# Queries of two attention heads laid block-diagonal with zeros, one 128-row product for both heads' scores

## The chip, the cores and the metric

The kernel runs on one core of one Trainium2 chip. The metric is the device time of one execution in microseconds (us), and the figure for the kernel before is the median of three runs. Matrix products run on TensorE, whose records in the trace come in two kinds: PEld, the load of the stationary operand (the weights), and PE, the product itself, which streams the columns of the moving operand past those weights. The other engines are VectorE (DVE), ScalarE (ACT), GpSimd (POOL) and SyncE (SP), which here issues most loads.

## The reference

Attention with a causal window of 64 over 8 sequences of 576 tokens, 8 heads of 64, and behind it a mixture of 8 experts that picks one expert for each token. What is computed:

```python
scores = scale * np.matmul(q, k.transpose(0, 1, 3, 2))
rel = pos[:, None] - pos[None, :]
mask = (rel >= 0) & (rel < window)
scores = np.where(mask, scores, -1000000000.0)
attn = np.exp(scores - np.max(scores, axis=-1, keepdims=True))
attn = attn / (np.sum(attn, axis=-1, keepdims=True) + 1e-09)
x = np.matmul(attn, v)                       # to (B, S, H * D)
...
h = np.maximum(x[b, s] @ w1[e], 0.0)         # e: the expert chosen for this token
out[b, s] = p[e] * (h @ w2[e])
```

## The kernel before

The 4608 tokens are cut into nine stretches `sc` of 512 tokens (`SC`), and the 8 heads into four pairs `hp`. One `(sc, hp)` is a unit, so there are 36. For each unit `scores` (L387 on) makes S = K Q for both heads of the pair with keys on the partitions; the exponential is taken on ACT (L425), the window mask is multiplied in on DVE (L430; in the units of `BIASED` the mask is instead added by four or six short bf16 products, L409), and `values` (L432 on) multiplies with V on TensorE (L440) and divides by the sums on DVE (L445 to L450).

Head 2·hp lies on partitions 0 to 63 of the loaded tile, head 2·hp+1 on 64 to 127. So a score product contracts over 64 rows only, and the array is used as four quarters of 64 rows by 64 columns: `j` (the head) picks the rows, `c` (even or odd block of 64 keys) the columns:

```python
def one(j, c, kt, block, a, b):
    h = slice(j * DH, (j + 1) * DH)
    nc.tensor.matmul(sp[j][c * WIN:(c + 1) * WIN, a:b], lhsT=kt[h, hp, block * WIN:(block + 1) * WIN],
                     rhs=qt[h, hp, a:b], start=not biased, stop=True, skip_group_check=biased)
```

Each unit has 18 such products, which the trace shows as 36 records (two for every float32 product). `sp[j]` is one PSUM bank for each head, out of a pool of three.

The order on TensorE, ACT and SP is the order in which the code is written: scores are made two units ahead (`LEAD`), that is, in the turn of unit i the scores of i+2 come first and then the values of i. Between them stand transposes and gate products (L310, L323, L325, L340) and pieces of the router, which `step` deals out. DVE and POOL are ordered by the scheduler.

Keys and queries are loaded together: the array `kq` holds for each stretch and partition the four pairs' keys and queries side by side, one tile of 2 MB is filled in two halves by L240 on SP's queue, and lies in the pool `ring` of four buffers, which the experts' weights `w1` and `w2` use later (`weights`, L1257). `va` (L235) is V with a column of ones, `vtt` (L230) V turned around for the gates. Behind attention the experts run block by block (L1279, L1357, L1408, L1508 are their products).

Of the kernel before, what the change touches and what calls it, by code (L numbers as in the profile page):

```python
# [8 lines left out]
F32 = mybir.dt.float32  # L9
# [74 lines left out]
def kernel(  # L84
# [36 lines left out]
    xs = xs, xw  # L121
    moe = xs, (w1, w1t), w2, out, tabs, lt, ident
    with ExitStack() as fast:
        ring = fast.enter_context(tc.tile_pool(name="ring", bufs=4))
        rt = Router(fast, tc, lt, xs, tabs, ident)
        ex = Experts(fast, tc, ring, *moe)
        zeros, n = ex.xp.tile([P, D], F32, name="xg"), (ZR - T1) // HF
        nc.vector.memset(zeros[:HF], 0.0)

        def small():  # L130
            nc.gpsimd.dma_start(out=wgs, in_=wg)
            nc.gpsimd.dma_start(out=wg2s, in_=wg2)
            for i in (ZR, N + 1):
                nc.gpsimd.dma_start(out=xs[0][i:i + 1, :], in_=zeros[:1])
                nc.gpsimd.dma_start(out=xw[i:i + 1, :], in_=zeros[:1, :PW])
            nc.gpsimd.dma_start(out=xw[T1:ZR, :].rearrange("(c p) o -> p c o", p=HF),
                                in_=zeros[:HF, :n * PW].rearrange("p (c o) -> p c o", c=n))

        attention(tc, ring, kq, v3, v4, vt, vh, xs[0], lt, ok, wgs, wg2s, ident, rt, ex, small)
        ex.run(fast, rt, lambda ps: flag(nc, ps, ok, bad, tabs["ej"][:, NBLK:], rare, ident))  # L140
    if_rare = nc.values_load(rare[0:1, 0:1], min_val=0, max_val=1,  # L141
                             skip_runtime_bounds_check_because="the larger of two comparisons")
    with tc.If(if_rare > 0):
        if_bad = nc.values_load(bad[0:1, 0:1], min_val=0, max_val=1,
                                skip_runtime_bounds_check_because="the result of a comparison")
        with tc.If(if_bad > 0):
            careful(tc, q, k, v, xs[0], lt, wgs, ident)
            with ExitStack() as slow:
                ring = slow.enter_context(tc.tile_pool(name="ring2", bufs=4))
                rt = Router(slow, tc, lt, xs, tabs, ident)  # L150
                rt.prepare()
                ex = Experts(slow, tc, ring, *moe)
                with tc.tile_pool(name="rt_ps1", bufs=1, space=PSUM) as ps:
                    for _ in rt.first(lambda: ps.tile([P, SC], F32, name="a")):
                        pass
                ex.begin()
                ex.run(slow, rt)
        if_more = nc.values_load(tabs["ej"][0:1, NBLK:], min_val=0, max_val=1,
                                 skip_runtime_bounds_check_because="the larger of two comparisons")
        with tc.If(if_more > 0), ExitStack() as slow:  # L160
            ring = slow.enter_context(tc.tile_pool(name="ring3", bufs=4))
            Experts(slow, tc, ring, *moe).more(slow)


# [10 lines left out]
def attention(ctx, tc, ring, kq, v3, v4, vt, vh, xs, lt, ok, wg, wg2, ident, rt, ex, small):  # L175
# [34 lines left out]

    ctx.enter_context(tc.manual_schedule(engines={ET.PE, ET.Activation, ET.SP}))

    kqs, qts, kts, vts, vas, vbs = {}, {}, {}, {}, {}, {}

    def width(sc):
        return VW if sc in GATED else VX
# [9 lines left out]
    def load(sc, parts):  # L226
        for part in parts:
            if part == "turned":
                vts[sc] = tp.tile([P, HP, SC], F32, name="vtt")
                nc.sync.dma_start(out=vts[sc], in_=vt[GATED.index(sc)])  # L230
            elif isinstance(part, tuple):
                if sc not in vas:
                    vas[sc] = space("va", sc)
                src, h = v4[GATED.index(sc)] if sc in GATED else v3[sc], slice(*part)
                nc.sync.dma_start(out=vas[sc][:, :, h], in_=src[:, :, h])  # L235
            else:
                if sc not in kqs:
                    kqs[sc] = ring.tile([P, HP, 2, SC], F32, name="w")
                    kts[sc], qts[sc] = kqs[sc][:, :, 0], kqs[sc][:, :, 1]
                nc.sync.dma_start(out=kqs[sc][:, part], in_=kq[sc, :, part])  # L240

    late = cp.tile([1, 4], F32, name="late")

# [29 lines left out]

    colf = columns()
    masks = []

    def build_mask(i):
        m = cp.tile([P, KB, 2, WIN], F32, name=f"mask{i}")
# [106 lines left out]
        return copied  # L385

    def scores(sc, hp):  # L387
        qt, kt = qts[sc], kts[sc]
        sp = [ps_s.tile([P, SC], F32, name="sp") for _ in range(2)]
        biased = (sc, hp) in BIASED  # L390

        def one(j, c, kt, block, a, b):
            h = slice(j * DH, (j + 1) * DH)
            nc.tensor.matmul(sp[j][c * WIN:(c + 1) * WIN, a:b], lhsT=kt[h, hp, block * WIN:(block + 1) * WIN],  # L394
                             rhs=qt[h, hp, a:b], start=not biased, stop=True, skip_group_check=biased)

        first = -sc * KB % SB
        if biased:
            for n in range(2):
                for c in range(2):  # L400
                    for j in range(2):
                        h, a = slice(j * DH, (j + 1) * DH), slice(0, SC)
                        x = bias[h, c].rearrange("p b i q -> p (b i q)")
                        if n:

                            if first >= KB or c == first % 2:
                                continue
                            a, x = slice(first * WIN, (first + 1) * WIN), never[h]
                        nc.tensor.matmul(sp[j][c * WIN:(c + 1) * WIN, a], lhsT=unit[h], rhs=x, start=not n, stop=False,  # L409
                                         skip_group_check=True)  # L410
        for s in range(5):
            for c in range(2):
                for j in range(2):
                    if c == 0:
                        if s < 4:
                            one(j, 0, kt, 2 * s, s * P, (s + 1) * P)
                    elif s:
                        one(j, 1, kt, 2 * s - 1, s * P - WIN, min(s * P + WIN, SC))
                    elif sc:
                        one(j, 1, kts[sc - 1], KB - 1, 0, WIN)  # L420
                    else:
                        one(j, 1, kt, 1, 0, WIN)
        p = pp.tile([P, 2, SC], F32, name="p")
        for j in range(2):
            nc.scalar.activation(p[:, j], sp[j], Act.Exp, scale=DH ** -0.5)  # L425
        if biased:
            return p
        a = 0 if sc == KB else (MID[sc % 2] - sc) * WIN
# [30 lines left out]
            shift_first(0)  # L459
    warm(6)  # L460
    until(0, masks[0][:1, :1])
    load(1, [pairs[0], whole, pairs[1]])
    moves, gated, turned, old = (), None, None, None
    side = None
    pause, trip = 0, False
# [13 lines left out]
    for i, (sc, hp) in enumerate(units):  # L479
# [33 lines left out]
        if i == 0:  # L513
            second = shift_first(1)
            until(1, allr[:1, 0, 0, 0, :1])
            load(2, [pairs[0], whole, pairs[1]])
            nc.sync.dma_start(out=vhs, in_=vh)
            load(3, pairs)
        if i == 2:
            with tc.issue_after(second.ins):  # L520
                small()
        if i == 2 * HP:
            with tc.issue_after(masked[-1].ins):
                rt.prepare()
# [641 lines left out]
class Experts:  # L1166
# [82 lines left out]
    def weights(self, st, n, names=("w1", "w2"), behind=lambda: None):  # L1249
# [4 lines left out]
        for name, w, a, b in (("w1", self.w1[not st["plain"]], DK, F), ("w2", self.w2, FK, D)):  # L1254
            if name not in names:
                continue
            t = self.ring.tile([P, a * b], F32, name="w")  # L1257
# [483 lines left out]
```

## Time and profile before

| what | value |
| --- | --- |
| median of the runs | 630.11 us (627.29 to 633.33) |
| time of the profiled execution | 631.83 us |
| its span, first to last instruction | 630.1 us |
| TensorE clock granted over the span | 0.996 |
| DMA over the span | 165.80 MB, mean 263 GB/s |

Attention takes the first 134 us of the span: the experts' first transposes (L1279) stand on TensorE from 132.27, the last unit's values from 133.31, and the experts' first products (L1508) begin at 134.50. The page's first part gives for each engine the time in which an instruction was in flight. For TensorE that is an upper bound of its work, since the ends of products are modelled and overlap the next ones; how densely it really works is read from the starts of consecutive blocks in the timeline.

### The profile page before, as it was taken

The page shows a single profiled execution, that of the slowest core. Times are in us where ns is not written, and L with a number is a line of the kernel's source. Part 1 is how long each engine was busy: PE and PEld are TensorE (multiplying, and loading weights), DVE is VectorE, ACT ScalarE, POOL GpSimd, SP SyncE. Part 2 cuts the span into 40 slices and gives each one's busy share as a digit, 9 for nine tenths or more (in the row PEclk, how much of TensorE's full clock was granted, in tenths as well). Part 3 has the DMA queues.
Part 4 walks back from the last instruction along what each step waited for, and adds up shares of the span by engine and source line. Part 5 has one row for each costly group of instructions (what it writes and reads, how often), then busy time and mean ns, then how long its engine had stood idle before and what let it go on. Part 6 is the DMA issues. An engine that isn't in the chain of part 4 may idle for free. (4 is left out here: it accounts for less than half of the span.)

```text
span 630.1 us, 15072 instructions
## 1 busy us (share of the span) xinstructions
PE 604.0 (96%) x6253; PEld 530.7 (84%) x6253; DVE 402.1 (64%) x757; ACT 200.7 (32%) x368; POOL 275.5 (44%) x261
## 2 busy tenths in 40 slices
PE   8897988999999999999999999999999999999995
PEld 7676766788889998979898889888997998989994
DVE  5667569888986867346472785183927753886730
ACT  3756655632482131203130213022211221213120
POOL 4532111532103567448165873174375765462001
PEclk9999999999999999999999999999999999999998
DMA  8999898886945566487966765678678656965501
GB/s 319 397 419 400 326 377 298 287 319 238 384 154 202 185 227 250 165 295 248 403 244 236 304 221 208 225 305 318 284 262 320 225 186 240 374 217 208 197 18 39
DMA packets 31880, 165.80 MB, mean 263 GB/s; under 512 B 10531, under 2 KB 12217, under 8 KB 22586
## 3 DMA queue, kind: packets, MB, share of 16 engines
q1 hardware_dynamic: 20394, 135.54, 57.9%
q0 software_dynamic: 11408, 29.20, 13.0%
q8 instruction: 51, 0.84, 0.5%
q14 instruction: 27, 0.22, 0.1%
HBM read 145.52 MB, written 19.59 MB: 262 GB/s over the span
## 5 line engine op out<-in xcount | busy, mean ns | idle before, releaser
L1184 POOL DMA_INDIRECT xg<-xs,g x118 | 139.1, 1179 | 46.5 <-issue 25.6
L1488 POOL DMA_INDIRECT out_dram<-y,idx x36 | 40.8, 1133 | 159.0 <-DVE y L1419 69.9
L1408 PE MATMUL hp<-ws,hs 128*128 128x256 f32 x384 | 88.9, 380 | 0.0
L1408 PEld LDWEIGHTS hp<-ws,hs 128*128 128x128 f32 x384 | 72.6, 190 | 10.9 <-issue 1.2
L1357 PE MATMUL hp<-xs,ws 128*128 128x128 f32 x672 | 79.7, 275 | 0.0
L1357 PEld LDWEIGHTS hp<-xs,ws 128*128 128x128 f32 x672 | 77.3, 192 | 0.1
L1508 PE MATMUL hp<-xt,w 128*64 128x64 f32 (+2 forms) x640 | 66.2, 276 | 0.0
L1508 PEld LDWEIGHTS hp<-xt,w 128*128 128x128 f32 (+1 forms) x640 | 60.8, 170 | 4.1 <-issue 0.7
L1419 DVE SCALAR_TENSOR_TENSOR y<-hp,pws,kept 128x256 f32<-128x256 f32 x48 | 22.1, 480 | 63.5 <-issue 38.1
L1408 PE MATMUL hp<-w,h 128*128 128x256 f32 x256 | 60.5, 379 | 0.0
L1369 DVE TENSOR_TENSOR h<-hp,keep 128x512 f32<-128x512 f32 x42 | 28.6, 690 | 44.0 <-PE hp L1357 43.2
L1357 PEld LDWEIGHTS hp<-xt,w 128*128 128x128 f32 x448 | 53.2, 192 | 2.7 <-issue 2.3
L1357 PE MATMUL hp<-xt,w 128*128 128x128 f32 x448 | 54.7, 275 | 0.0
L394 PEld LDWEIGHTS sp<-w 64*64 64x64 f32 x1296 | 39.9, 139 | 16.1 <-issue 11.5
L1408 PEld LDWEIGHTS hp<-w,h 128*128 128x128 f32 x256 | 47.3, 190 | 5.7
L394 PE MATMUL sp<-w 64*64 64x128 f32 (+1 forms) x1296 | 45.8, 272 | 5.7 <-issue 4.2
L425 ACT ACTIVATE p<-sp 128x512 f32<-128x512 f32 x72 | 39.1, 595 | 37.6 <-PE sp L394 35.2
L440 PE MATMUL xo<-vb,p 128*64 128x74 f32 (+1 forms) x576 | 45.0, 230 | 5.5 <-DVE x L450 2.2
L430 DVE TENSOR_TENSOR p<-p,mask 128x1024 f32<-128x1024 f32 x29 | 35.6, 1227 | 22.6 <-ACT p L425 22.5
L1184 POOL DMA_INDIRECT pws<-xw,gx x40 | 43.7, 1093 | 13.1 <-issue 9.8
L440 PEld LDWEIGHTS xo<-vb,p 128*64 128x64 f32 x576 | 39.2, 139 | 9.7 <-issue 4.0
L1320 DVE TENSOR_TENSOR ws<-w 128x1024 f32<-128x1024 f32 x32 | 39.1, 1224 | 11.5 <-PE hp L1408 9.6
(287 smaller groups left out, 967.3 us busy)
## 6 DMA issues: line engine op xcount, KB each, us to landing
w<-in_w_dram SPq DMA_DIRECT2D x22, 2048.0 KB, 9.4
w<-in_w1t_dram SPq DMA_DIRECT2D x20, 2048.0 KB, 8.9
w<-in_kq_dram SPq DMA_DIRECT2D x17, 1024.0 KB, 10.4
w<-in_w_dram SPq DMA_DIRECT2D x24, 512.0 KB, 8.3
xs<-x POOLq DMA_DIRECT2D x9, 1024.0 KB, 7.0
va<-in_v_dram SPq DMA_DIRECT2D x5, 1184.0 KB, 5.3
vtt<-in_vt_dram SPq DMA_DIRECT2D x5, 1024.0 KB, 6.3
va<-in_v_dram SPq DMA_DIRECT2D x3, 1040.0 KB, 14.2
```

The source lines that it names most:

```text
L394: nc.tensor.matmul(sp[j][c * WIN:(c + 1) * WIN, a:b], lhsT=kt[h, hp, block * WIN:(block + 1) * WIN], rhs=qt[h, hp, a:b], start=not biased, ...
L425: nc.scalar.activation(p[:, j], sp[j], Act.Exp, scale=DH ** -0.5)
L430: masked.append(nc.vector.tensor_tensor(p, p, m.to_broadcast([P, 2, SC]), op=Alu.mult))
L440: nc.tensor.matmul(xo[par * WIN:(par + 1) * WIN, j, s * VW:s * VW + n], lhsT=p[:, j, b * WIN:(b + 1) * WIN], rhs=w[:, s, 2 * hp + j, :n], ...
L1184: return self.nc.gpsimd.indirect_dma_start(out=out, out_offset=None, in_=table[:rows, :], in_offset=bass.IndirectOffsetOnAxis(ap=idx, axis=0))
L1320: self.nc.vector.tensor_tensor(o, x, y, op=sub)
L1357: mm = nc.tensor.matmul(out[:, m, :], lhsT=a[:, kk, m * P:(m + 1) * P], rhs=b[:, kk, :], start=start and m + kk == 0, stop=stop and (m, kk ...
L1369: nc.vector.tensor_tensor(o, x, y, op=add)
L1408: mm = nc.tensor.matmul(out, lhsT=a[:, m, :], rhs=b[:, m, :], start=start and m == 0, stop=stop and m == FK // 2 - 1, skip_group_check=True)
L1419: nc.vector.scalar_tensor_tensor(o, x, pw[i], y2, Alu.mult, Alu.add)
L1488: return self.nc.gpsimd.indirect_dma_start(out=self.out[:, :], out_offset=bass.IndirectOffsetOnAxis(ap=st["idx"][:, s:s + 1], axis=0), in_ ...
L1508: mm = nc.tensor.matmul(hp[a, i, :], lhsT=st["w1"][:, kk, m * P:(m + 1) * P][:, a], rhs=st["xt"][:, kk, :n], start=(kk == 0), stop=(kk == ...
```

## The change

Three things are done. First, the queries of a pair now lie block-diagonal: a tile `[128, pair, j, hp, 512]` holds head 2·hp's queries on partitions 0 to 63 at `j` = 0 and head 2·hp+1's on 64 to 127 at `j` = 1, and zeros elsewhere. There are two such tiles for the whole of attention, used in turn by even and odd stretches; the zeros are written once by `clear`. Second, a score product contracts over all 128 rows (64 of keys of each head) and streams both heads' queries, `[2, 128]` or `[2, 64]` columns, so one product gives both heads' scores; the array is used as two halves of 128 rows by 64 columns. A PSUM bank now holds both heads' scores of half the stretch (256 queries) where it held one head's of the whole. Third, keys and queries are loaded apart: keys of two stretches share one `w1` buffer (those of the last stretch have a tile of their own), the two query tiles are the two `w2` buffers, and `ring` has two buffers for each of the names in place of four for one.

```diff
-        ring = fast.enter_context(tc.tile_pool(name="ring", bufs=4))
+        ring = fast.enter_context(tc.tile_pool(name="ring", bufs=2))
...
+    turns = [ring.tile([P, 2, 2, 2, SC], F32, name="w2") for _ in range(2)]
+    turns.reverse()
+    for sc in range(NSC):
+        qts[sc] = turns[sc % 2]
+    def clear(sc, pair, hps, engines):
+        for j, e in enumerate(engines):
+            e.memset(qts[sc][j * DH:(j + 1) * DH, pair, 1 - j, hps], 0.0)
+    clear(0, 0, slice(0, 1), (nc.gpsimd, nc.vector))
...
+            elif isinstance(part, slice):
...
+                nc.sync.dma_start(out=kts[sc][:, part], in_=kq[sc, :, 0, part])
             else:
-                if sc not in kqs:
-                    kqs[sc] = ring.tile([P, HP, 2, SC], F32, name="w")
-                    kts[sc], qts[sc] = kqs[sc][:, :, 0], kqs[sc][:, :, 1]
-                nc.sync.dma_start(out=kqs[sc][:, part], in_=kq[sc, :, part])
+                pair, hps = part if isinstance(part, list) else (part, slice(0, 2))
+                for j in range(2):
+                    h, e = slice(j * DH, (j + 1) * DH), nc.scalar if (sc, pair, hps.stop) == (0, 0, 1) else nc.sync
+                    e.dma_start(out=qts[sc][h, pair, j, hps],
+                                in_=kq[sc, h, 1, 2 * pair + hps.start:2 * pair + hps.stop])
...
-    load(0, [slice(0, 1), slice(1, 2), (0, H // 2), pairs[1], (H // 2, H)])
+    load(0, [[0, slice(0, 1)], slice(0, 1), slice(1, 2), [0, slice(1, 2)], (0, H // 2), pairs[1], 1, (H // 2, H)])
...
+    clear(0, 0, slice(1, 2), (nc.gpsimd, nc.vector))
+    clear(0, 1, slice(0, 2), (nc.gpsimd, nc.gpsimd))
+    clear(1, 0, slice(0, 2), (nc.gpsimd, nc.gpsimd))
...
-        sp = [ps_s.tile([P, SC], F32, name="sp") for _ in range(2)]
+        sp = [ps_s.tile([P, 2, half], F32, name="sp") for _ in range(2)]
...
-        def one(j, c, kt, block, a, b):
-            h = slice(j * DH, (j + 1) * DH)
-            nc.tensor.matmul(sp[j][c * WIN:(c + 1) * WIN, a:b], lhsT=kt[h, hp, block * WIN:(block + 1) * WIN],
-                             rhs=qt[h, hp, a:b], start=not biased, stop=True, skip_group_check=biased)
+        def one(c, kt, block, a, b):
+            i = a // half
+            nc.tensor.matmul(sp[i][c * WIN:(c + 1) * WIN, :, a - i * half:b - i * half],
+                             lhsT=kt[:, hp, block * WIN:(block + 1) * WIN], rhs=qt[:, :, a:b],
+                             start=not biased, stop=True, skip_group_check=biased)
...
+        for b in range(KB):
+            if b % 2 == 0:
+                one(0, kt, b, b * WIN, (b + 2) * WIN)
+            lo = b * WIN
+            if b == 0:
+                one(1, *((kts[sc - 1], KB - 1) if sc else (kt, 1)), 0, WIN)
+            elif b % 2 and (lo + WIN) % half:
+                one(1, kt, b, lo, lo + 2 * WIN)
+            elif b % 2:
+                one(1, kt, b, lo, lo + WIN)
+                if b + 1 < KB:
+                    one(1, kt, b, lo + WIN, lo + 2 * WIN)
...
-        for j in range(2):
-            nc.scalar.activation(p[:, j], sp[j], Act.Exp, scale=DH ** -0.5)
+        for i in range(2):
+            nc.scalar.activation(p[:, :, i * half:(i + 1) * half], sp[i], Act.Exp, scale=DH ** -0.5)
...
         if 0 < sc < NSC - 2 and hp == 0:
-            load(sc + 2, [whole])
-        if 0 < sc < NSC - 3 and hp == 1:
-            load(sc + 3, pairs)
+            load(sc + 2, [whole, 0])
+        if sc and sc % 2 == 0 and sc + 2 < NSC and hp == 1:
+            load(sc + 2, [slice(0, HP)])
+        if 0 < sc < NSC - 2 and hp == 2:
+            load(sc + 2, [1])
...
+        if sc and sc % 2 == 0 and sc + 3 < NSC and hp == 3:
+            load(sc + 3, [slice(0, HP)])
```

On TensorE, this is the scores block of one unit of the first stretch with its two neighbours, the kernel before (a row names the destination, its operands and the shape written; `w` is the tile of keys and queries):

```order
L440 MATMUL xo<-va,p 64x65
L394 MATMUL sp<-w 64x128 x2
L394 MATMUL sp<-w 64x64 x2
L394 MATMUL sp<-w 64x128 x12
L394 MATMUL sp<-w 64x64 x2
L440 MATMUL xo<-vb,p 64x65
```

And the same block in the changed kernel (`w_129` is the even query tile, `w_138` the keys of the first two stretches):

```order
L465 MATMUL xo<-va,p 64x65
L417 MATMUL sp<-w_129,w_138 64x2x128
L417 MATMUL sp<-w_129,w_138 64x2x64
L417 MATMUL sp<-w_129,w_138 64x2x128 x2
L417 MATMUL sp<-w_129,w_138 64x2x64 x2
L417 MATMUL sp<-w_129,w_138 64x2x128 x3
L417 MATMUL sp<-w_129,w_138 64x2x64
L465 MATMUL xo<-vb,p 64x65
```

Eighteen products of up to 128 columns have become ten of up to 256; the place of the block between the values of two units is the same.

On SP, these are the loads of one round in the middle of attention, the kernel before:

```order
L235 DMA va<-in_v_dram 128x2368
L240 DMA w<-in_kq_dram 128x2048 x2
L230 DMA vtt<-in_vt_dram 128x2048
L235 DMA va<-in_v_dram 128x2368
L240 DMA w<-in_kq_dram 128x2048 x2
L230 DMA vtt<-in_vt_dram 128x2048
```

And in the changed kernel (`w_128` and `w_129` are the query tiles, `w_785` keys):

```order
L246 DMA va<-in_v_dram 128x2368
L259 DMA w_129<-in_kq_dram 64x1024 x2
L254 DMA w_785<-in_kq_dram 128x2048
L259 DMA w_129<-in_kq_dram 64x1024 x2
L241 DMA vtt<-in_vt_dram 128x2048
L254 DMA w_785<-in_kq_dram 128x2048
L246 DMA va<-in_v_dram 128x2368
L259 DMA w_128<-in_kq_dram 64x1024 x4
L241 DMA vtt<-in_vt_dram 128x2048
```

The queries of a stretch come as four loads of half the partitions each, behind `va` and on both sides of the keys, where keys and queries came as two loads of whole tiles.

On POOL, the start of the kernel before, up to the copies of V that the first values read:

```order
masks.py:197 MEMSET ident 128x128
L263 ISA
L263 IOTA row 128x1
masks.py:199 AFFINE_SELECT ident<-ident 128x128
L270 IOTA p 128x512
L382 MEMSET vb 64x520
L383 COPY vb<-va 64x4x260
```

And in the changed kernel:

```order
masks.py:197 MEMSET ident 128x128
L222 MEMSET w_129 64x512
masks.py:199 ISA
masks.py:199 AFFINE_SELECT ident<-ident 128x128
L283 IOTA row 128x1
L290 IOTA p 128x512
L222 MEMSET w_129 64x512
L222 MEMSET w_129 64x1024 x2
L222 MEMSET w_128 64x1024 x2
L405 MEMSET vb 64x520
L406 COPY vb<-va 64x4x260 x2
```

Six clears of the query tiles now stand ahead of the memset and the copy of `vb`.

More of the change, by code (lines that the diff above doesn't have):

```diff
@@ L235, in load @@
                 nc.sync.dma_start(out=vas[sc][:, :, h], in_=src[:, :, h])
[L236 to L240 removed]
+            elif isinstance(part, slice):
+                if sc not in kts:
+                    if sc == NSC - 1:
+                        kts[sc] = cp.tile([P, HP, SC], F32, name="last")
+                    else:
+                        both = ring.tile([P, 2, HP, SC], F32, name="w1")
+                        kts[sc], kts[sc + 1] = both[:, 0], both[:, 1]
+                nc.sync.dma_start(out=kts[sc][:, part], in_=kq[sc, :, 0, part])
+            else:
+                pair, hps = part if isinstance(part, list) else (part, slice(0, 2))
[3 more added lines that the diff above has]
+                                in_=kq[sc, h, 1, 2 * pair + hps.start:2 * pair + hps.stop])
     late = cp.tile([1, 4], F32, name="late")
@@ L400, in scores @@
                 for c in range(2):
-                    for j in range(2):
-                        h, a = slice(j * DH, (j + 1) * DH), slice(0, SC)
-                        x = bias[h, c].rearrange("p b i q -> p (b i q)")
+                    for i in range(2):
+                        h, a, w = slice(i * DH, (i + 1) * DH), 0, half
+                        x = bias[h, c].rearrange("p b i q -> p (b i q)")[:, i * half:(i + 1) * half]
                         if n:
-                            if first >= KB or c == first % 2:
+                            if first >= KB or c == first % 2 or i != first * WIN // half:
@@ L407, in scores @@
                                 continue
[L408 to L422, printed above, removed]
+                            a, w, x = first * WIN - i * half, WIN, never[h]
@@ new lines, in scores @@
+                        nc.tensor.matmul(sp[i][c * WIN:(c + 1) * WIN, :, a:a + w], lhsT=unit[h],
+                                         rhs=x.rearrange("p (o q) -> p o q", o=1).to_broadcast([DH, 2, w]),
+                                         start=not n, stop=False, skip_group_check=True)
+        for b in range(KB):
[10 more added lines that the diff above has]
+                    one(1, kt, b, lo + WIN, lo + 2 * WIN)
@@ L423, in scores @@
         p = pp.tile([P, 2, SC], F32, name="p")
-        for j in range(2):
-            nc.scalar.activation(p[:, j], sp[j], Act.Exp, scale=DH ** -0.5)
+        for i in range(2):
+            nc.scalar.activation(p[:, :, i * half:(i + 1) * half], sp[i], Act.Exp, scale=DH ** -0.5)
         if biased:
@@ L461, in attention @@
     until(0, masks[0][:1, :1])
-    load(1, [pairs[0], whole, pairs[1]])
+    load(1, [pairs[0], 0, whole, pairs[1], 1])
     moves, gated, turned, old = (), None, None, None
@@ L515, in attention @@
             until(1, allr[:1, 0, 0, 0, :1])
-            load(2, [pairs[0], whole, pairs[1]])
+            load(2, [slice(0, HP), whole, 0])
             nc.sync.dma_start(out=vhs, in_=vh)
-            load(3, pairs)
+            load(3, [slice(0, HP)])
+        if i == 1:
+            load(2, [1])
         if i == 2:
@@ L1720 @@
         "v": v.reshape(N, D),
-        "kq": _np.stack([by_sc(turned(i[n])) for n in "kq"], 3),
+        "kq": _np.stack([by_sc(turned(i[n])) for n in "kq"], 2),
         "v3": v3,
```

11 lines of the change are left out of this document (6 added, 5 removed).

## The prediction

> **What bounds the kernel now.** I read the windows first (busy time of each engine in a stretch), then TensorE's timeline inside attention, then its waits. Two stretches, columns as named in the header:
>
> ```profile
> core 0: us, PE busy (x) PEld busy (x) DVE busy (x) ACT busy (x) POOL busy (x), PEclk, DMA share, GB/s
> 20.00:120.00 100.00, 87.20 (x2057) 70.57 (x2047) 70.05 (x191) 63.74 (x107) 26.93 (x34) 1.00 0.94 355
> 132.00:630.00 498.00, 487.89 (x3583) 434.88 (x3578) 308.71 (x525) 121.04 (x234) 232.10 (x203) 0.99 0.66 240
> ```
>
> Behind attention TensorE is busy in 488 of 498 us; the change leaves the products there alone, so I carry that part over. In attention TensorE is busy 87 of 100 us and no other engine is above 70, but the DMA share is 0.94, so loads could be the bound as well. The timeline of TensorE decides (start, duration, records; in brackets the idle time and what ended it):
>
> ```profile
> 42.92 0.27 PE L440 MATMUL xo<-vb,p 128*64 128x65 f32 x1 [0.68 <-issue]
> ...
> 43.62 0.22 PE L440 MATMUL xo<-va,p 128*64 128x65 f32 x1
> 43.77 1.12 PE L394 MATMUL sp<-w 64*64 64x128 f32 x36
> 44.81 0.27 PE L440 MATMUL xo<-vb,p 128*64 128x65 f32 x1
> ...
> 44.92 0.22 PE L440 MATMUL xo<-vb,p 128*64 128x65 f32 x1
> ...
> 45.74 0.22 PE L440 MATMUL xo<-vb,p 128*64 128x65 f32 x1
> 45.75 0.22 PE L440 MATMUL xo<-va,p 128*64 128x65 f32 x1
> 45.90 1.06 PE L323 MATMUL r<-p,wgs 128*32 128x512 f32 x8
> 46.89 1.09 PE L394 MATMUL sp<-w 64*64 64x128 f32 x28
> 49.11 0.55 PE L394 MATMUL sp<-w 64*64 64x128 f32 x8 [1.13 <-issue]
> ```
>
> Block follows block without a hole: a scores block takes 43.77 to 44.81 = 1.04 us, a values block 44.81 to 45.90 = 1.09. What holes there are, the waits name for the same 100 us (total, times, longest):
>
> ```profile
> PE sp L394 <- issue: 4.2, 4, 1.6
> PE xo L440 <- issue: 2.9, 4, 1.4
> PE xo L440 <- DVE x L450: 2.2, 3, 1.4
> PE xo L440 <- ACT p L313: 1.2, 2, 0.7
> PE r L840 <- DVE loc L835: 0.9, 1, 0.9
> PE r L830 <- ACT va L356: 0.6, 1, 0.6
> PE r L998 <- ACT va L356: 0.5, 1, 0.5
> PE xo L310 <- ACT p L313: 0.2, 1, 0.2
> ```
>
> None of them is a load. So attention goes at TensorE's pace, with 7.1 us of "issue" and 5.6 us of waits for DVE and ACT in it: time added to TensorE there comes out at the end, less what those holes give back.
>
> **The scores, the main term.** Before, four quarters of the array work at once, each streaming the 512 columns of one head for one parity of key blocks, in two records per product. Now two halves work at once, each streaming 2 x 512 columns. The work per record must be priced. Two tiles of 128 rows by 64 do run at once today: `vb` and `va` records start within 0.01 us of each other (45.74 and 45.75), and the 14 steps of `vb` from 44.92 to 45.74 give 0.0586 us for a 65-column record, 0.90 ns a column. L323 has four tiles of 128x32, two 512-column records each, in 45.90 to 46.89; less a block's edge (1.09 − 16 × 0.0586 = 0.15) that is 0.42 us a record, 0.82 ns a column. A record of just the new width stands in the experts, with twice the weights to load:
>
> ```profile
> L1408 PE MATMUL hp<-w,h 128*128 128x256 f32 x256 | 60.5, 379 | 0.0
> ```
>
> 60.5 / 256 = 0.236 us. So a 256-column record costs between 0.210 and 0.236; a unit's half has eight of them (the halves with 128-column records have as many columns), so a block costs 8 × 0.210 + 0.15 = 1.83 to 8 × 0.236 + 0.15 = 2.04. I take 0.215, near L323, whose tiles are narrow like the new ones: 1.87 us. Minus 1.04 that is +0.83 a unit, and × 36 units **+29.9 us** (28.4 to 36.0).
>
> **The edges of blocks.** A block that cuts the array in another way than the one before starts later than one that keeps the cut:
>
> ```profile
> 64.70 0.66 PE L340 MATMUL r<-ident,gs 128*128 128x128 f32 x4
> 65.29 0.27 PE L440 MATMUL xo<-vb,p 128*64 128x65 f32 x1
> ...
> 68.80 0.66 PE L340 MATMUL r<-ident,gs 128*128 128x128 f32 x4
> 69.29 0.93 PE L310 MATMUL xo<-ident,x 128*128 128x128 f32 x7
> ```
>
> The same four transposes give way after 0.59 us to values (128x64) and after 0.49 to other transposes (128x128): 0.10 for a change of cut. Scores and values now share one cut, and they stand side by side some 32 times in the built order: **−3.2 us** (0 if the wait for the exponential at the edge holds it anyway). The seven units with bias products keep 64x64 for those and gain a change between them and the scores: +0.7.
>
> **The start.** The first two units run at half speed:
>
> ```profile
> 5.01 2.39 PE L394 MATMUL sp<-w 64*64 64x128 f32 x38 [0.69 <-DMA w<-in_kq_dram]
> 7.73 1.98 PE L394 MATMUL sp<-w 64*64 64x128 f32 x34 [0.33 <-ACT p L425]
> 9.64 1.54 PE L256 MATMUL r<-ident 128*128 128x128 f32 x6
> ```
>
> 36 records take about 2 us here against 1.04 later, so each of these two units grows by twice 0.83: another **+1.7**. The first half of the scores is now a bank of its own that the exponential can start on in the middle of the block, which hides part of it, so 0 to 2.
>
> **The clears, and the loads that are moved.** POOL's rows at the start:
>
> ```profile
> 2.05 0.53 POOL L382 MEMSET vb<- 64x520 f32 x1
> 8.84 1.49 POOL L383 COPY vb<-va 64x1040 f32<-64x1040 f32 x1 [6.27 <-DMA va<-in_v_dram]
> ```
>
> Six clears, two of 64x512 and four of 64x1024, are 2 × 0.53 + 4 × 1.05 = 5.3 us ahead of that copy, which waited 6.27 us for `va`; so they fit, with 1 us to spare, and were the cover gone, the copy and the first values would be late by that. DVE's two clears (about 1 us) stand ahead of the masks. On SP and ACT's queue the first unit's 512 KB come as four loads, and `va` stands two places later. For all this I put **+1.0**, between 0 and 3.
>
> In the middle, what is queued on SP waits as follows, and lands in (second view, DMA issues: KB each, median us):
>
> ```profile
> SPq L235 <- PE xo L440: 34.7, 6, 11.3
> SPq L240 <- PE sp L394: 18.6, 5, 4.7
> ...
> w<-in_kq_dram SPq DMA_DIRECT2D x10, 1024.0 KB, 8.2
> ```
>
> Pair 0's queries for stretch sc+2 go out behind `va`, whose own wait (for the last values of sc−1) ends later than that for the scores they overwrite, so their wait is nothing new. Pair 1's queries wait for the scores of (sc, 3) and hold up `vtt` and the keys behind them by about a unit. They are wanted six units later, at some 3.5 us a unit 21 us, against 8.2 to land. I cost this at 0; if that cover went, the wait would show as PE waiting for `in_kq`. ACT's exponentials are as many elements as before and DVE's masks are unchanged: 0.
>
> **What the holes give back.** The stops called "issue" come in the midst of blocks, and every 128 records: from 42.92 to 49.11 there are 24 records of values, 36, 32, 8 and 28 = 128. A queue of the DMA view has the same beat:
>
> ```profile
> q8 instruction: 17, 0.28, 1.1%
> DMA packets 7989, 35.46 MB, mean 355 GB/s; under 512 B 2939, under 2 KB 2955, under 8 KB 4672
> ```
>
> Seventeen packets in these 100 us for 2057 records is one for 121, in 16 KB pieces (0.28 MB / 17): TensorE waits for its next instructions while loads take 355 GB/s. Now a unit has 20 scores records where it had 36, and takes 0.8 us longer, so 128 records last some 8 us instead of under 6; a stop of about 1 us (7.1 / 8) is then covered. I take **−7.1** (0 to −9), and half of the 5.6 us of waits for DVE and ACT, which get more time per unit: **−2.8** (0 to −5.6).
>
> [...]
>
> **Sum.** 29.9 − 3.2 + 0.7 + 1.7 + 1.0 − 7.1 − 2.8 = **+20.2 us**. The profiled execution took 631.83 us (span 630.1), which gives 652; the median of the runs is 1.7 lower, 630.11, which gives **650**. A measurement of this kernel tells about 1% (6.3 us) from no change. With the ends of the terms, the case runs from about +11 to +32.
>
> **Rivals.**
> - *The holes stay.* The stops are not the fetch's, or the new waits make up for them (clears, `va` late, queries late): 630.1 + 29.9 − 3.2 + 0.7 + 1.7 + 1.0 = 660. For it: waits of SP's queue are long; against it: the beat of 128 records. Chance 0.14.
> - *Records start in the written order.* Then a record for a busy half holds up the next for the free one. The new order c0, c1, c1, c0, c1, c1, c0, c1, c0, c1 with two records each would need 19 slots of 128 columns where free halves need 16, 3 × 0.105 × 36 = 11 us more: 661. Against it: the old order would by the same rule take 17 slots, 1.8 us, and takes 1.04. Chance 0.06. [...]
> - *Attention is bound by its loads* (DMA share 0.94), and longer products go into holes: 630, no change. Against it: no load is among the waits of those 100 us. Chance 0.04.
> - *Records, not columns, are the price.* 36 records in 1.04 us are 29 ns each; were that the bound, 20 would take 0.58, 0.46 × 36 = 17 us less: **613**, faster. It decides if a 256-column record costs a half under 0.13 us (1.04 / 8). Against it: L323's 8 records take 0.99 us, and L1408's 0.236 each. Chance 0.03.
> - *The halves do not run at once* when a record streams two heads, so the change loses both its cuts: 16 × 0.215 = 3.4 a block, about 36 × 1.7 = 62 more: 712. The pairs of `vb` and `va` speak against it. Chance 0.01.
>
> **How the numbers follow.** The forecast has 0.72 and gives the time, 650. Its own ends are 641 to 662; the first two rivals lie at 660 and 661, inside it or at its edge; the other three, 0.08, lie outside, so the range is 641 to 662. Faster by over 1%: 0.03 (the fourth rival). Within 1%: 0.05 (the third and a forecast whose holes all close). Slower by over 1%: 0.92.
>
> **What would show it.** In the changed kernel's profile: 720 scores records of 64 columns by 128 rows, and blocks of 1.83 to 2.04 us (under 1.1 or over 3: a rival is right); "issue" under 3 us in attention; the experts' first products at about 154 instead of 134.5, and the part behind them as long as before. PE waiting for `in_kq` or `vb` would show that a cover is gone, and a part behind attention that is more than 3 us longer or shorter would show that I was wrong to carry it over.

## The result, and the profile after

The changed kernel takes 650.82 us (median of 4 runs, 648.01 to 655.93) against 629.3 for the kernel before in the same runs: 1.0343 times as long, with an interval of 1.026 to 1.0426. Its profiled execution took 650.77 us with a span of 648.7.

The windows of the changed kernel (busy time of each engine; the first two rows answer to 20 to 120 us and to 132 to 630 us of before):

```profile
20.00:120.00 100.00, 93.34 (x1394) 70.99 (x1391) 60.47 (x161) 58.22 (x93) 24.33 (x33) 0.97 0.98 316
150.00:648.00 498.00, 487.67 (x3572) 434.65 (x3570) 308.08 (x523) 121.15 (x234) 227.76 (x203) 1.00 0.65 240
...
38.00:50.00 12.00, 12.00 (x179) 8.89 (x177) 6.39 (x10) 5.38 (x11) 0.00 (x0) 0.87 0.97 209
```

Behind attention nothing changed (487.67 busy in 498 us, 487.89 before); the experts' first products start at 153.21 instead of 134.50, so attention holds the whole loss. In it TensorE is busier (93 for 87 of 100 us). The last two columns ask for attention: the DMA share is as high as before (0.98 for 0.94), yet the loads move 316 GB/s instead of 355, and from 38 to 50 us only 209. The kernel before, same view:

```profile
38.00:50.00 12.00, 10.19 (x231) 8.23 (x229) 9.17 (x34) 7.94 (x14) 5.38 (x13) 1.00 1.01 419
```

TensorE's waits in 20 to 120 us of the changed kernel (total, times, longest):

```profile
PE sp L417 <- DMA w<-in_kq_dram: 3.0, 1, 3.0
PE xo L465 <- ACT p L336: 2.5, 1, 2.5
PE xo L465 <- issue: 0.5, 1, 0.5
```

The stops called "issue" went from 7.1 to 0.5 us. In their place stand one wait for keys and queries and one for ACT, which itself waits 2.87 us for `va` there. The timeline of TensorE shows the start, the two waits and a clean block:

```profile
6.57 5.52 PE L417 MATMUL sp<-w,w 128*64 128x256 f32 x40 [1.87 <-DMA w<-in_kq_dram]
...
28.07 3.28 PE L417 MATMUL sp<-w,w 128*64 128x256 f32 x20 [3.00 <-DMA w<-in_kq_dram]
...
37.66 0.37 PE L465 MATMUL xo<-vb,p 128*64 128x65 f32 x1 [2.45 <-ACT p L336]
...
58.92 0.27 PE L465 MATMUL xo<-vb,p 128*64 128x65 f32 x1
...
59.91 1.91 PE L417 MATMUL sp<-w,w 128*64 128x256 f32 x20
61.75 0.30 PE L383 MATMUL r<-ident,ahead 128*64 128x128 f32 x1
```

A clean scores block takes 59.91 to 61.75 = 1.84 us, and the values ahead of it 58.92 to 59.91 = 0.99 instead of 1.09: the edge between two blocks of one cut is 0.10 cheaper. The block at 28.07 takes 3.28 where the clean one's row has 1.91, and the windows of the two stretches behind the waits show why, in the column PEclk:

```profile
27.50:30.80 3.30, 2.73 (x17) 2.24 (x19) 0.00 (x0) 0.60 (x1) 0.00 (x0) 0.50 1.01 335
37.70:41.00 3.30, 3.30 (x40) 1.97 (x40) 2.03 (x3) 1.51 (x3) 0.00 (x0) 0.50 1.08 225
```

In each the granted clock is half for 3.3 us or more; the first of the two stretches begins while TensorE still waits. The work in it takes longer by 1.4 us after the first wait (the block takes 28.07 to 31.29 = 3.22 for 1.84) and by some 1.7 after the second (half of 3.3 or more, an estimate).

### The profile page after: what moved, and what is told of

It is laid out like the page before. It is cut to its first block, busy times and chain, and to the rows that moved or that the text cites. A ratio compares the mean times of both kernels' runs of the same rounds, so it can differ in the third digit from the quotient of the medians.

```text
span 648.7 us, 13962 instructions
## 1 busy us (share of the span) xinstructions
PE 627.1 (97%) x5670; PEld 544.3 (84%) x5670; DVE 407.8 (63%) x759; ACT 204.9 (32%) x368; POOL 275.3 (42%) x269
## 5 line engine op out<-in xcount | busy, mean ns | idle before, releaser
L1216 POOL DMA_INDIRECT xg<-xs,g x118 | 137.8, 1168 | 48.9 <-issue 24.4
L1520 POOL DMA_INDIRECT out_dram<-y,idx x36 | 39.4, 1094 | 157.4 <-DVE y L1451 67.4
L417 PE MATMUL sp<-w,w 128*64 128x256 f32 (+1 forms) x648 | 66.5, 351 | 4.9 <-DMA w<-in_kq_dram 4.9
L417 PEld LDWEIGHTS sp<-w,w 128*64 128x64 f32 x648 | 49.3, 142 | 22.1 <-issue 12.5
L450 ACT ACTIVATE p<-sp 128x512 f32<-128x512 f32 x72 | 42.6, 597 | 44.1 <-PE sp L417 42.5
L1216 POOL DMA_INDIRECT pws<-xw,gx x40 | 41.8, 1045 | 14.8 <-issue 7.0
L465 PE MATMUL xo<-vb,p 128*64 128x74 f32 (+1 forms) x576 | 43.4, 229 | 3.2 <-ACT p L336 2.5
L1402 ACT ACTIVATE h<-h 128x512 f32<-128x512 f32 x42 | 26.3, 630 | 60.0 <-DVE h L1401 60.0
```

The costliest lines, as they stand in the source:

```text
L417: nc.tensor.matmul(sp[i][c * WIN:(c + 1) * WIN, :, a - i * half:b - i * half], lhsT=kt[:, hp, block * WIN:(block + 1) * WIN], rhs=qt[:, :, ...
L450: nc.scalar.activation(p[:, :, i * half:(i + 1) * half], sp[i], Act.Exp, scale=DH ** -0.5)
L465: nc.tensor.matmul(xo[par * WIN:(par + 1) * WIN, j, s * VW:s * VW + n], lhsT=p[:, j, b * WIN:(b + 1) * WIN], rhs=w[:, s, 2 * hp + j, :n], ...
L1216: return self.nc.gpsimd.indirect_dma_start(out=out, out_offset=None, in_=table[:rows, :], in_offset=bass.IndirectOffsetOnAxis(ap=idx, axis=0))
L1402: nc.scalar.activation(o, x if y is None else o, Act.Relu)
L1520: return self.nc.gpsimd.indirect_dma_start(out=self.out[:, :], out_offset=bass.IndirectOffsetOnAxis(ap=st["idx"][:, s:s + 1], axis=0), in_ ...
```

## The experiments

The times are ratios to the kernel before in runs on the same chip. Runs 5 to 8 were on another chip than the rest, on which the kernel before takes 644.91 us.

The theory at first was that of the prediction: the longer products cost the time, and the loads little. The rival was that the loads that were cut up cost it. The first four runs undo or vary one part each.

**1. The quarter products on the new loads.** The products of before read the block-diagonal tile:

```diff
-        def one(c, kt, block, a, b):
+        def one(j, c, kt, block, a, b):
+            h = slice(j * DH, (j + 1) * DH)
+            nc.tensor.matmul(sp[j][c * WIN:(c + 1) * WIN, a:b], lhsT=kt[h, hp, block * WIN:(block + 1) * WIN],
+                             rhs=qt[h, j, a:b], start=not biased, stop=True, skip_group_check=biased)
```

> The changed kernel with the score products of the kernel before: 64 rows contracted, four quarters, one PSUM bank per head, reading the same block-diagonal tile (its zeros are not read), with the new loads and clears. Theory (the columns that the products stream are the price): scores blocks fall back from 1.84 to about 1.05 us, the edges of 0.10 us come back, and so do the stops every 128 records; what is left over the kernel before is only what the new loads cost at the start (waits for in_kq and for va, and the half clock behind them), so 632 to 640 us. Rival (the new loads are the larger cost): 643 us or more. Second rival (loads cost nothing): 627 to 631.

Measured: 648.7 us, ratio 1.029 (1.0235 to 1.0345), in the range of the rival (643 or more). The quick blocks are back (64.70 to 65.86 = 1.16 us, behind a stop of 2.32) and almost nothing is won. TensorE's waits in 0 to 155 us:

```profile
PE sp L417 <- issue: 13.3, 7, 2.9
PE xo L463 <- issue: 4.1, 3, 2.4
```

The stops that the changed kernel had lost are more than twice as long as before (17.4 for 7.1 us). So the new loads, with the clears and the new buffers that this run keeps, cost nearly as much as the whole change, and the theory as put falls.

**2. One head for each product.** Twice as many records of half the columns, on the new loads:

```diff
+            for j in range(2):
+                nc.tensor.matmul(sp[i][c * WIN:(c + 1) * WIN, j, a - i * half:b - i * half],
+                                 lhsT=kt[:, hp, block * WIN:(block + 1) * WIN], rhs=qt[:, j, a:b],
```

> The changed kernel with every score product cut in two, one for each head, still over 128 rows with the zeros: as many columns streamed, but 40 records a unit where there are 20. Theory (columns are the price): the warm scores block stays at 1.83 to 1.90 us. If the stops every 128 records in the kernel before were the fetch of instructions under load, some of them come back, since 128 records now last about 6.5 us: total 651 to 658 us, with 1 to 6 us of issue in attention. Rival (records are the price, or a floor per record): block 2.2 us or more and the total above 663. Rival on the stops (they were something else): no issue, total 651.

Measured: 656.68, ratio 1.0417 (1.0369 to 1.0464), and issue stops of 5.9 us are there again, both as expected. A block takes 1.99 us for 40 records, over the 1.83 to 1.90 of the theory and under the 2.2 of the rival, so records have a small price of their own. The edit doubles the records and leaves the columns as they are, so the stops go with the records.

**3. Fewer loads in the second stretch.** Six loads of keys and queries joined to three, of up to 1 MB:

```diff
+            elif part == "Q":
+                for j in range(2):
+                    h = slice(j * DH, (j + 1) * DH)
+                    nc.sync.dma_start(out=qts[sc][h, :, j], in_=kq[sc, h, 1].rearrange("d (a b) s -> d a b s", a=2))
...
-    load(1, [pairs[0], 0, whole, pairs[1], 1])
+    load(1, [slice(0, HP), "Q", whole])
```

> The changed kernel with the loads of the second stretch joined: one for the keys, one per head for the queries, then V, four loads where there were seven; the same bytes. Theory (the new small loads hold each other up at the start, since a load waits for the one eight places ahead of it, and the waits for in_kq of 3.0 us and for va of 2.5 us with the half clock behind them came from that): the wait for in_kq goes, the clock stays up, 643 to 648 us. Rival (the start is bound by the bytes and the small packets alone): the wait moves to another load, 649 to 653 us.

Measured: 648.08, ratio 1.0299 (1.0265 to 1.0334), at the border of the two ranges expected. The interval overlaps that of the changed kernel, so the gain is not settled. What the waits show is a move: TensorE's wait of 2.5 us for ACT is gone, and that for keys and queries has grown to 7.1 us, 4.7 in one piece. The eight places of the theory are in the waits of SP's queue in the changed kernel: the loads of queries that go out at 14.30, 23.10 and 35.51 us waited 1.0, 4.3 and 4.5 us for a `va`, and the `va` loads of 6.45, 10.54 and 17.17 stand eight places ahead of them.

**4. All products of even blocks first.** The two halves of the array then stand apart in the program:

```diff
+        for b in range(0, KB, 2):
+            one(0, kt, b, b * WIN, (b + 2) * WIN)
         for b in range(KB):
-            if b % 2 == 0:
-                one(0, kt, b, b * WIN, (b + 2) * WIN)
```

> The changed kernel with the four even-block products of a unit written first and the six odd-block ones behind them, so that the two halves of the array are no longer written in turn. If a record starts when its own half is free, as far ahead as all ten products of a unit reach, the block stays at 1.84 us and the total at 651. If records start strictly in the written order, the halves work one after the other for most of the block: about 3.4 us a block, and 651 + 36 x 1.5 = 705 us. In between: reordering reaches only some records ahead.

Measured: 669.93 (one run), between the two numbers expected. The timeline of TensorE:

```profile
61.81 2.82 PE L417 MATMUL sp<-w,w 128*64 128x256 f32 x20
64.56 0.30 PE L383 MATMUL r<-ident,ahead 128*64 128x128 f32 x1
```

The block takes 61.81 to 64.56 = 2.75 us. The groups of the scores line by shape (busy, mean ns of one), one row from the stretch of 61.8 to 62.675 us and one from that of 62.5 to 62.68:

```profile
L417 PE MATMUL sp<-w,w 128*64 128x256 f32 x5 | 1.2, 379 | 0.0
```

```profile
L417 PE MATMUL sp<-w,w 128*64 128x128 f32 x1 | 0.3, 323 | 0.0
```

The even blocks are eight records of 256 columns, and the first record of the odd blocks, of 128, is the ninth in the program. Up to 62.675 us five of 256 have started and none of 128; by 62.68 the first of 128 runs. So it starts right behind the fifth and overtakes three records that wait for the other half, in this block of this one run. In the changed kernel's alternating order a block takes 1.84.

**5 and 6. Longer packets.** What is it in the new loads? First guess: packets of 4 KB and below, where before most had 8 or more (in 20 to 100 us 3940 of 5648 packets are under 8 KB, in the kernel before 2394 of 5352). The query tile is turned to `[row, head, pair, query]`, so that from the second stretch on one load brings a head's 512 KB in rows of 8 KB; once with the new products, once with the quarters:

```diff
-    turns = [ring.tile([P, 2, 2, 2, SC], F32, name="w2") for _ in range(2)]
+    turns = [ring.tile([P, 2, HP, SC], F32, name="w2") for _ in range(2)]
...
+            elif part == "Q":
+                for j in range(2):
+                    h = slice(j * DH, (j + 1) * DH)
+                    nc.sync.dma_start(out=qts[sc][h, j], in_=kq[sc, h, 1])
```

> The changed kernel with longer packets: queries are kept [row, head of the pair, pair of heads, query], and from the second stretch on one load brings all 512 KB of a head (64 rows of 8 KB), and the second stretch's keys come in one load. Theory (the 256 KB loads in 4 KB packets move less at a time, so keys, queries and values come late in the first third, and each stop of 2.5 to 3 us brings half clock after it): the waits for in_kq and va between 6 and 40 us go, and the time is 643 to 649. Rival (the whole stretch's queries now go out in one go behind the last scores of the stretch before, so they land no earlier, or the wait moves to the keys): 650 or more. Blocks of 1.83 us in both.

> The loads of the run above, with the quarter products of the kernel before (64 rows by 64 columns, block 1.05 us). The quarters on the changed kernel's own loads took 648.7 with 17 us of issue stops. Theory A (4 KB packets lengthen the fetch of instructions): the stops shrink to the kernel before's 7 us and the time is 629 to 637. Theory B (it is the loads that reach only 64 rows, half of the memory's rows at a time, or the mere number of bytes under way): stops of 12 us or more stay and the time is 640 to 650.

Measured: 1.0316 (1.0239 to 1.0394) and 1.0396 (1.032 to 1.0472). Neither got quicker; with the new products the waits for keys and queries come to 12.9 us, and with the quarters issue stops of 19.7 us stay. Longer packets don't help; but these loads also go out later, all of a stretch's queries at once, so the size alone is tried next.

**7. Smaller packets in the kernel before.** The other way round: keys and queries loaded apart, each with 128 rows:

```diff
-                nc.sync.dma_start(out=kqs[sc][:, part], in_=kq[sc, :, part])
+                for t in range(2):
+                    nc.sync.dma_start(out=kqs[sc][:, t, part], in_=kq[sc, :, t, part])
```

> The kernel before, with keys and queries loaded apart: two loads of 128 rows for each one of before, packets of half the size (4 KB for 8 KB), the products unchanged. Theory A (small packets or more loads slow the fetch of instructions): issue stops of 11 us or more in attention for 7.1, and 636 to 648. Theory B (it is the loads to 64 rows that do it): stops as before, and 627 to 633.

Measured: 1.0003 (0.9963 to 1.0042), issue stops of 5.2 us. Twice as many loads in packets half as long cost nothing, as theory B had it.

**8 and 12. The new products on the old loads.** The products of 128 rows by 64 columns read the old query tile with the pair's queries repeated at stride 0. The zeros are left out, so the products have the shape and number of the changed kernel's and the scores are not the right ones:

```diff
-        qt, kt = qts[sc], kts[sc]
+        qt, kt, half = qts[sc][:, hp], kts[sc], SC // 2
...
+                             lhsT=kt[:, hp, block * WIN:(block + 1) * WIN], rhs=qt[:, a:b].rearrange("p (o q) -> p o q", o=1).to_broadcast([P, 2, b - a]),
```

> The kernel before with its own loads and its own query tile, and the changed kernel's products of 128 rows by 64 columns: the queries are not block-diagonal, each product reads the same queries twice (stride 0 over the pair), so both heads get the sum of the two heads' scores. No clears. Theory (products and loads each cost about 19 alone, and overlap together since longer products cover the fetch): block 1.83, no issue stops, and 645 to 650, within 5 of the changed kernel. Rival (the costs add: products +16 or less and the rest loads): 640 to 644.

> A repeat of the halves on the loads of the kernel before (each product reads the same queries twice, so both heads get the sum of the two heads' scores; no clears), which took 1.0083 of the kernel before on another chip than the first runs. If that holds here: 1.005 to 1.015, and the experts' first products at 142 to 144 us. If it was the chip: 1.02 or more, as the theory of the run had it.

Measured: 1.0083 (1.0045 to 1.012), and on the first chip 638.88 us, 1.013 (1.0095 to 1.0165). Applied to 629.3 us, these ratios are 635 and 637 us beside the changed kernel's 651, under the 645 to 650 expected of the products alone and under the rival's 640 to 644 too; the repeat came out as expected. The products are the smaller part. The windows of the second run, whole attention and then the stretch from above:

```profile
0.00:142.05 142.05, 137.73 (x2138) 108.69 (x2138) 97.77 (x243) 84.71 (x136) 40.09 (x58) 1.00 0.89 333
...
38.00:50.00 12.00, 12.00 (x205) 9.49 (x203) 9.67 (x36) 7.82 (x12) 5.41 (x13) 1.00 1.02 421
```

TensorE idles for 4.3 of 142.05 us, at the full clock, with loads at 421 GB/s where the changed kernel has 209 (over 20 to 100 us, 374 for 316).

**9. The halves of the queries on two queues.** What is left of the loads is that a head's queries reach 64 rows. If two such loads run together, they reach 128:

```diff
-                    h, e = slice(j * DH, (j + 1) * DH), nc.scalar if (sc, pair, hps.stop) == (0, 0, 1) else nc.sync
+                    h, e = slice(j * DH, (j + 1) * DH), nc.scalar if j or (sc, pair, hps.stop) == (0, 0, 1) else nc.sync
```

> The changed kernel, with the loads of the second head's queries (rows 64 to 127) on ACT's queue instead of SP's, so that the two loads of a pair, 64 rows each, can be under way together. Theory (loads that reach 64 rows move at half the rate, 209 GB/s from 38 to 50 us of the changed kernel's profile at a DMA share of 0.97; two such loads at once reach all 128 rows): the DMA moves over 350 GB/s in that stretch, the waits for in_kq and va shrink, and the time is 1.008 to 1.02 of the kernel before. Rival (the rate has to do with something else, or ACT stands behind its own load issues): 1.03 or more.

Measured: 650.68, ratio 1.0315 (1.0269 to 1.0361): no help, with 8.3 us of waits for keys and queries. Over 20 to 100 us the loads move 319 GB/s where the changed kernel has 316. From 38 to 50 us it is 309, under the 350 expected; that it is more than 209 says little, since a short stretch varies: run 1 has 393 from 35.35 to 42.10 us with the changed kernel's own loads.

**10 and 11. The loads of before, cut by rows.** Nothing else is touched, in run 10 on one queue, in run 11 with rows 64 to 127 on ACT's:

```diff
-                nc.sync.dma_start(out=kqs[sc][:, part], in_=kq[sc, :, part])
+                for j in range(2):
+                    h = slice(j * DH, (j + 1) * DH)
+                    nc.sync.dma_start(out=kqs[sc][h, part], in_=kq[sc, h, part])
```

> The kernel before with nothing changed but that each load of keys and queries goes out as two loads of 64 rows each, on the same queue; packets of the same size and number, same products. Theory (64-row loads move at half the rate): the quarter products on the changed kernel's loads, with 1 MB a stretch in such loads, cost 18 us; here it is 2 MB, so 1.04 to 1.065 of the kernel before, issue stops of 12 us or more, and 250 to 320 GB/s in 20 to 100 us. Rival (it was the order or the number of loads of the changed kernel): 1.015 or less.

> As the run above, but rows 64 to 127 on ACT's queue, so that both halves can be under way together. Theory: the rate comes back (over 350 GB/s in 20 to 100 us) and the time is 0.995 to 1.02 of the kernel before; what ACT waits for its own load issues is the uncertain part. Rival (as slow as the run above): 1.04 or more.

Measured: 671.48 us, ratio 1.0613 (1.0553 to 1.0674), and 674.24, 1.0696 (1.0648 to 1.0744). The same bytes in packets of the same size cost 6% when each load reaches half the rows; that there are twice as many loads is not it, by run 7. A second queue doesn't mend it (in run 11 a single wait of 19.4 us for ACT blurs the time, but the loads too move only 269 GB/s in 20 to 100 us). The windows of run 10:

```profile
20.00:100.00 80.00, 54.82 (x1065) 43.69 (x1065) 34.30 (x69) 34.89 (x58) 17.09 (x29) 0.85 1.02 275
```

The loads move 275 GB/s at a DMA share of 1.02; the kernel before has 380 at 0.98 there. One expectation missed: issue stops are 6.4 us, not 12 or more; the time is lost in waits for the loads themselves (17.9 us) and for ACT (13.6). TensorE's waits in 0 to 155 us:

```profile
PE xo L442 <- ACT p L315: 13.6, 3, 8.0
PE r L327 <- DMA vtt<-in_vt_dram: 10.0, 3, 4.3
PE sp L396 <- DMA w<-in_kq_dram: 7.9, 7, 2.0
PE xo L442 <- issue: 4.2, 4, 1.4
```

The rate can be read from the queue that carries these loads (packets, MB, share of 16 engines). In 20 to 100 us of the kernel before, of run 7, of the changed kernel and of run 10, in this order:

```profile
q1 hardware_dynamic: 3844, 24.92, 79.7%
```

```profile
q1 hardware_dynamic: 6004, 25.95, 83.1%
```

```profile
q1 hardware_dynamic: 4329, 20.79, 85.4%
```

```profile
q1 hardware_dynamic: 3172, 18.51, 87.5%
```

Bytes by share × 80 us × 16 engines: one engine moves 24.4 GB/s with loads of 128 rows, whether in long packets or in short (run 7, 24.4 too); 19.0 where a part of the bytes goes to 64 rows, and 16.5 where all keys and queries do. In run 10 some 18 loads of 512 KB, 9.4 of the 18.5 MB, are such loads: with the rest at 24.4 they had 1120 − 372 = 748 us of engine time, 12.6 GB/s, half the rate (an estimate, since loads issued in the window need not land in it, and the rest may be slower too). ACT's queue can be read without that assumption, since in 20 to 100 us of runs 11 and 9 it carries nothing but loads of 64 rows (in this order):

```profile
q10 hardware_dynamic: 893, 5.83, 31.6%
```

```profile
q10 hardware_dynamic: 877, 2.87, 12.4%
```

That is 14.4 and 18.1 GB/s an engine. So loads of 64 rows are slower in every one of these runs, by a quarter to a half; the exact rate is not settled.

The totals in 20 to 100 us are lower too, on one queue (run 10, 275 GB/s) and on two (runs 9 and 11, 319 and 269), for 380 in the kernel before. Why loads of 64 rows are slower, no run shows.

## Why the prediction was right, and for which wrong reasons

The time was forecast as 650 and is 650.82, and what the profile was to show is there: 720 scores records, blocks of 1.84 us, "issue" at 0.5, experts at 153.21, the same work behind. But that the number came out so close is luck: TensorE's added work and the loads were each off by some 10 us, in opposite directions. The account of attention is TensorE's busy time up to the experts' first product, from the windows of the kernel before, run 1 and the changed kernel (run 12's stands above):

```profile
0.00:134.50 134.50, 118.65 (x2721) 98.00 (x2722) 95.44 (x239) 80.71 (x136) 43.36 (x58) 1.00 0.92 347
```

```profile
0.00:152.62 152.62, 124.23 (x2721) 102.22 (x2721) 100.52 (x241) 80.80 (x136) 48.72 (x66) 0.93 0.92 306
```

```profile
0.00:153.21 153.21, 141.72 (x2138) 111.37 (x2139) 102.37 (x245) 84.94 (x136) 47.57 (x66) 0.98 0.96 309
```

In the table the scores and values rows are from the windows of that line alone, and "other" is what is left of the busy time. Ends of scores and values that overlap a neighbour are thereby taken from "other", so these three rows are good to a few us; busy time as a whole and idle time are firmer. Run 1 has with the new loads also the clears and the new buffers.

| us | before | products alone (12) | loads without products (1) | changed kernel |
| --- | --- | --- | --- | --- |
| experts' first product at | 134.50 | 142.05 | 152.62 | 153.21 |
| scores | 45.77 | 70.58 | 46.92 | 72.66 |
| values | 45.40 | 42.87 | 47.76 | 43.97 |
| other | 27.48 | 24.28 | 29.55 | 25.09 |
| idle | 15.85 | 4.32 | 28.39 | 11.49 |

- *The scores, +29.9, with the start, +1.7.* The block came as forecast, 1.84 for 1.87. The term is mis-sized all the same: products alone raise the scores by 70.58 − 45.77 = 24.8, not 31.6. The step that failed is "minus 1.04": a clean block stood for all 36. The line's busy time of before, 45.77 / 36 = 1.27 where a clean block's row has 1.12, already held blocks stretched by stops and by a slow start, which shrink with the change; run 12 has 1.96, near its clean 1.91. Half speed at the start did not double the loss: the first two units take 4.87 to 9.79 in run 12 against 5.01 to 9.64, 0.3 us more, since the half speed also ends earlier. The six transposes behind them show it, which take 1.54 us at 9.64 in the kernel before and 0.87 in run 12 (this half speed is read from the length of the records; the column PEclk has 1.00 there):

```profile
9.79 0.87 PE L256 MATMUL r<-ident 128*128 128x128 f32 x6
```

- *Edges, −3.2 + 0.7 = −2.5.* The price is right, 0.10 us for an edge. That the values line is 2.5 us shorter in run 12 doesn't show the whole term: its first block, at half speed in the kernel before, alone goes from 1.93 us (11.11 to 13.04) to 0.98 (10.59 to 11.57).
- *"Other".* It falls by 3.2 in run 12, but that is no work saved: the lines L310, L323, L325 and L340 are each busy as long as before (8.6, 4.3, 5.3 and 5.9 us in the kernel before and in run 8, the same kernel as run 12), and the transposes L256 by 0.7 less (4.4 and 3.7). All of TensorE's busy time grows by 137.73 − 118.65 = 19.1 us, where the scores, the start and the edges were put at 29.1.
- *What the holes give back, −9.9.* Right in kind and nearly in size: idle time falls by 11.5 in run 12. That the stops belong to the fetch of instructions fits all runs with products that use 128 records faster or slower (runs 1 and 2 with stops of 17.4 and 5.9 us, and run 12), though no run shows that a fetch ended one of them. In run 12 TensorE's waits name no "issue" of more than 0.2 us.
- *The clears.* Right: the copy behind them waits 0.83 us for `va` and is not late by them.
- *The loads that are moved, +1.0 with the clears, between 0 and 3.* This is the step that failed most: "I cost this at 0". From run 12 to the changed kernel attention grows by 153.21 − 142.05 = 11.2 us, of it 7.2 idle and 4.0 busy, which is mostly the work at half clock behind the two waits (1.4 and 1.7 us); the ratios say 1.0343 − 1.013 = 2.1%, 13 us. The start is part of it: the first unit begins at 6.57 us, in run 12 at 4.87. I considered the order on the queue, and took 8.2 us to land from 1 MB loads that reach all 128 rows; the new ones reach 64, and though they have a quarter of the bytes, they land later, and the keys' loads of 128 rows behind them too (20 to 100 us of the changed kernel; KB each, median us):

```profile
w<-in_kq_dram SPq DMA_DIRECT2D x21, 256.0 KB, 14.9
w<-in_kq_dram SPq DMA_DIRECT2D x5, 1024.0 KB, 15.2
```

- *The sum.* Products alone give +7.6 in attention (8.2 by the ratio of 1.013), where the terms without loads and clears had 19.2; the loads give 11.2, where 1.0 stood. The upper end of the range, +32, is not the sum of the upper ends, which is 36.0 + 0.7 + 2 + 3 = 41.7: it takes for granted that the holes give back 9.9.
- *The rival "attention is bound by its loads"* was judged against because no load was among the waits. It names the right resource with the wrong consequence: the DMA engines were nearly always busy (share 0.94), so a change that lowers their rate, here from 355 to 316 GB/s in 20 to 120 us, costs time. The table shows it: once the new loads are in, quarters or halves hardly matter (152.62 or 153.21), though TensorE's work differs by 17.5 us. The two costs overlap and don't add: 7.6 and 18.1 alone, 18.7 together.

Left open is how the loads lengthen the issue stops in runs 1 and 11 (17.4 and 18.4 us) and not in run 10 (6.4): that instructions are fetched behind slower packets was the author's guess, and no run shows it. Nor does a run have the changed kernel's order and buffers with loads of 128 rows, so what part of the 11.2 us is the order, the buffers or the clears stays open; run 10 shows the cost of the rows in the kernel before, where besides them only the number of loads differs. Without a try stayed a kernel that keeps the block-diagonal tile but fills it from a load of 128 rows by copies on an engine; by run 12, which has no cost for such copies, it would still not beat the kernel before, and no run here did.

## What to carry to other kernels

Before a load is cut up, look at how many rows each piece reaches (here 12.6 to 18.1 GB/s an engine to 64 rows, 24.4 to 128), not only at its bytes and its place in the queue; a transfer price measured on another shape of load is a price for that shape alone (8.2 us to land for 1 MB to 128 rows, 14.9 for a quarter of it to 64). Where the DMA share is as high as here (0.94), a change that leaves the bytes alone can still cost time through the loads, and here it showed as GB/s that fell at a share as high (316 for 355, at 0.98 for 0.94). Take the baseline of a block from the line's total over all its blocks (1.27 us here, the clean one's row 1.12): a clean one overstates what is added, since the stops that it leaves out may be what the change gives back.

## What the runs showed of the hardware

- Loads that reach 64 rows moved 12.6 GB/s an engine by the estimate above (run 10), and 14.4 and 18.1 read from ACT's queue (runs 11 and 9), where loads of 128 rows moved 24.4; a second queue didn't bring the rate back. Packets of 4 KB instead of 8 KB to 128 rows lost nothing (24.4, run 7).
- With TensorE waits of 3.0 and 2.5 us came 3.3 us or more at half clock (PEclk 0.50 in two stretches), which cost some 1.4 and 1.7 us more (the second an estimate, half of 3.3 or more).
- In one block of run 4 a record for one half of the array started ahead of three older ones that go to the other half; that block took 2.75 us, where starts in the written order were put at 3.4.
